# Router logits copied by ScalarE, gate factors stored by rows behind the rows' stores, the last routing ahead of the first expert slot, and solved systems back in four transfers

## The chip, the cores and the metric

The kernel runs on one core of a Trainium2 chip. The time is device microseconds for one execution, taken as the median of several runs. TensorE (PE) does the matmuls, VectorE (DVE), ScalarE (ACT) and GpSimd (POOL) the elementwise work, and SyncE (SP), ScalarE and GpSimd issue the DMA transfers, which 16 DMA engines carry out. The engines run their instructions in the order of the program and wait for one another by semaphores.

## What is computed

Three stages follow one another: a delta-rule attention over 768 steps for 4 x 8 heads of 48, a two-layer network with squared ReLU, and a mixture of eight experts of which each token takes the one with the highest router logit. Cut to its core:

```python
for t in range(S):                                   # attention, S = 768, D = 48
    kt, vt, bt = (k_n[:, :, t], v[:, :, t], beta[:, :, t, None])
    y[:, :, t] = np.einsum('bhd,bhde->bhe', q[:, :, t], state)
    v_old = np.einsum('bhde,bhd->bhe', state, kt)
    state = state + bt[:, :, :, None] * np.einsum('bhd,bhe->bhde', kt, vt - v_old)

x = y.transpose(0, 2, 1, 3).reshape(3072, 384)
h = np.maximum(x @ w_in, 0.0)                        # first network, d_ff = 2048
x = h * h @ w_out

logits = x @ w_gate                                  # experts: E = 8, F = 1024
expert_idx = np.argmax(logits, axis=1)
gate_w = softmax(logits)[np.arange(N), expert_idx]
for e in range(E):
    mask = expert_idx == e
    out[mask] = gate_w[mask, None] * (np.maximum(x[mask] @ w1[e], 0.0) @ w2[e])
```

## The kernel before

The 768 steps are cut into 12 chunks of 64. Within a chunk the recurrence becomes two triangular systems of 32 steps per head, which are solved for all 32 heads side by side. The order of all instructions is fixed when the program is built: a main loop runs over the chunks `c` and, in each, over eight units `i` of the first network (`l1_unit`, `l2_unit`), and hangs steps of the other work between them by tables of due times (in sixteenths of a chunk's units; `PRE_AT`, `CHAIN_AT`, `ROUTE_AT`).

While chunk `c` goes through the network, two other chunks are prepared. `pre(c)` consists of `front` and `solve`. `front` turns keys and queries, forms the Gram matrices (`grams`, L392 and L393, PSUM tile `gm`), and carries the 32 x 32 diagonal blocks through DRAM into a layout with one system per partition: ScalarE issues four stores `dg<-gd` (L422), SyncE two loads `gl<-dg` (L430). `solve` runs 31 elimination steps on VectorE (L520, L525), stores the result (`dt<-pt`, L535, two transfers) and loads it back by head (`tt<-dt`, L545, eight transfers of 32 KB). `norms` (L504) brings the key norms by head with small matmuls against columns of the unit matrix. `chain(c)` then does the sequential part: it loads `ktok` (L284), and runs z, u and y matmuls (L583, L594, L610); `s_step` (L641) updates the state at the start of the next chunk and reads `ktok`.

`route(c)` follows when the second layer of chunk `c` is done. It copies the rows out of PSUM (`xr`, L724, ScalarE) and stores them to DRAM (`xs_d`, L727, four transfers on SyncE); turns them (L734), multiplies them by the router's weights (L742, PSUM tile `lp`, 8 columns), copies the logits into the table `lga` (L743, VectorE, one for each of two token tiles), finds each token's expert and, by the rank matmuls `rk` (L781 to L785), its place in the expert's list, and scatters the token's number into `list_d` (L793, GpSimd). `gates(c0, c1)` turns logits into gate factors (`ga`, one per partition and column) and stores them to `g_d` (L809, four transfers on SyncE, in which each element of 4 bytes goes to its own place).

The PSUM tiles `gm`, `lp`, `xp`, `z`, `u`, `y` and `rk` share one pool of four buffers in turn.

In the last chunk the experts begin. At `i == 0` `first_slots` picks the two fullest lists, the lists of two slots are loaded (`ids`, L1017), the first slot's weights follow (`raw`, L992 and L996, seven transfers, 3 MB), and the gate factors of chunks 0 to 9 are stored. At `i == 2` GpSimd gathers the rows of the two slots (`gather`, L1023, `xg<-xs_d`) and their gate factors (`gather_gate`, L1032). A gather waits for all stores to its table that stand before it in the program. Weights are split into a high and a low part by ScalarE (L972) and VectorE (L973), `split_w`; each raw buffer that this frees takes the next slot's load.

After the loop the first slot's rows are turned (`transposed`, L1045, then L1047 on ScalarE and L1048 on VectorE, high and low part `xgT`), `route(11)` begins, and `slot(0)` and `slot(1)` run: four units of first-layer groups `h` (L1059, 18 matmuls of 256 columns) and second-layer groups `y` (L1071, 12 matmuls of 384 columns). The rest of `route(11)` is spread over slot 0, at `i == 2` the last two chunks' gate factors are stored and the third slot's list is loaded and its rows and factors gathered (`ahead(0)`); slot 1 also computes the table of the later slots (`slot_table`). Slots 2 to 9 are then one branch each, wide (L1081, L1091) or narrow.

The lines that move the transfers in question:

```python
for u in range(2):                                   # solve, L541 to L545
    for hf in range(2):
        for x in range(2):
            r0 = quad(x, hf)
            (nc.gpsimd if c == 0 and x else nc.sync).dma_start(out=tt[r0:r0 + 32, u], in_=dtr[hf, x, u])
```

## Time and profile before

| what | value |
|---|---|
| median of 3 runs | 1021.74 us (1018.74 to 1023.69) |
| the profiled execution | 1019.3 us, span 1017.5 us |
| mean granted clock of TensorE | 0.957 of full |
| busy: PE, PEld (its weight loads) | 910.4 us (89%), 849.9 us (84%) |
| busy: DVE, ACT, POOL | 664.9 us (65%), 514.3 us (51%), 315.4 us (31%) |
| DMA, mean over the span | 113.82 MB, 112 GB/s |
| packets under 512 bytes | 241053 of 273021 |

The table is read from the top: one engine, TensorE, is busy in nearly nine tenths of the span, so the time is its work plus what it stands still or runs slowly. The first 100 us are a start-up in which VectorE and the transfers set the pace, from there to about 711 us runs the loop over the chunks, then the experts. "SPq" in the rows is SyncE's queue of DMA issues and "ACTq" ScalarE's; a row gives the start, the duration, the engine, the source line, the operation, the tiles (out<-in) with their shapes, how many instructions the row holds, and in brackets how long the engine stood idle before it and what released it.

### The profile page before, as it was taken

What the parts mean: (1) busy time and instruction counts of PE and PEld (TensorE: products, weight loads), DVE (VectorE), ACT (ScalarE), POOL (GpSimd) and SP (SyncE); (2) the same over time, 40 slices, a digit from 0 to 9 for tenths busy, and PEclk for the clock granted to TensorE, in tenths of its full rate; (3) what the DMA queues carried; (4) which work ended last, traced back from release to release, by engine and by line L of the source; (5) the groups of instructions that cost most, each with busy time, mean ns of one, the idle gap of its engine ahead of it and who ended that gap; (6) DMA issues with size and microseconds to landing.
All of it is one profiled execution on the core that took longest, in us unless ns stands there. A gap on an engine that the chain in (4) does not pass through costs nothing.

```text
span 1017.5 us, 28821 instructions
## 1 busy us (share of the span) xinstructions
PE 910.4 (89%) x11416; PEld 849.9 (84%) x11416; DVE 664.9 (65%) x2270; ACT 514.3 (51%) x1025; POOL 315.4 (31%) x322
## 2 busy tenths in 40 slices
PE   6267979999899999999999999999789999999995
PEld 5135868988898888888888988999779999998994
DVE  6987897584949495868686777424564554463653
ACT  5146755555354645454545555455444444464553
POOL 2020023333142424242424342210434334353231
PEclk9689889999899999999999999999899999999998
DMA  8899292535343443435342531218786555564764
GB/s 159 139 184 272 40 103 31 84 38 85 49 83 50 77 56 57 61 57 74 63 72 49 80 55 38 38 55 140 139 251 209 158 165 174 165 218 136 236 199 133
DMA packets 273021, 113.82 MB, mean 112 GB/s; under 512 B 241053, under 2 KB 259554, under 8 KB 272096
## 3 DMA queue, kind: packets, MB, share of 16 engines
q1 hardware_dynamic: 244176, 92.87, 43.3%
q0 software_dynamic: 7344, 15.17, 5.8%
q10 hardware_dynamic: 21344, 3.67, 2.2%
q8 instruction: 100, 1.64, 0.8%
q14 instruction: 57, 0.47, 0.2%
HBM read 95.01 MB, written 17.82 MB: 111 GB/s over the span
## 4 chain that ended last, share of the span: by engine, by line
PE 54%; DVE 18%; DMA 12%; issue 5%; SPq 5%; ACT 4%; POOL 1%; another core or an unknown queue 0%; ACTq 0%; DVEq 0%; POOLq 0%
PE h L682 12%; PE x L710 11%; PE h L1059 6%; PE y L1071 5%; DVE tmp L520 5%; DVE pt L525 4%; PE h L1081 4%; PE y L1091 3%; DVE kq L381 2%; DMA raw<-in_moe_w_dram 2%; PE gm L392 2%; DMA xs_d<-xr 2%; PE wa L1091 2%; DMA st<-in_q_dram 1%; DMA xg<-xs_d,ids 1%
## 5 line engine op out<-in xcount | busy, mean ns | idle before, releaser
L682 PE MATMUL h<-xt,win 128*128 128x256 f32 x1728 | 235.1, 291 | 6.0 <-issue 2.9
L710 PE MATMUL x<-wout,gt 128*128 128x384 f32 x1152 | 229.1, 347 | 2.7 <-issue 2.3
L682 PEld LDWEIGHTS h<-xt,win 128*128 128x128 f32 x1728 | 220.6, 195 | 12.4 <-issue 5.1
L710 PEld LDWEIGHTS x<-wout,gt 128*128 128x128 f32 x1152 | 200.9, 192 | 9.7 <-issue 6.9
L692 POOL TENSOR_TENSOR gt<-r,gt 128x512 fp32r<-128x512 f32 x80 | 103.7, 1296 | 320.5 <-ACT gt L688 216.5
L520 DVE TENSOR_TENSOR tmp<-pt,gl 128x60 f32<-128x60 f32 (+37 forms) x662 | 142.4, 254 | 1.8
L686 ACT ACTIVATE r<-h 128x512 f32<-128x512 f32 x96 | 57.4, 597 | 166.9 <-PE h L682 118.9
L525 DVE TENSOR_TENSOR pt<-pt,tmp 128x60 f32<-128x60 f32 (+37 forms) x662 | 135.1, 243 | 4.3 <-remote 3.0
L973 DVE TENSOR_TENSOR ew<-raw,ew 128x768 fp32r<-128x768 f32 (+1 forms) x98 | 102.3, 1069 | 9.2 <-ACT ew L972 8.5
L1059 PE MATMUL h<-xgT,ew 128*128 128x256 f32 x648 | 85.0, 287 | 7.5 <-issue 4.5
L1059 PEld LDWEIGHTS h<-xgT,ew 128*128 128x128 f32 x648 | 82.1, 195 | 9.8 <-issue 7.3
L972 ACT CAST ew<-raw 128x768 fp32r<-128x768 f32 (+1 forms) x98 | 87.4, 923 | 1.9 <-DMA raw<-in_moe_w_dram 1.9
L1071 PE MATMUL y<-ew,ht 128*128 128x384 f32 x432 | 86.3, 347 | 0.0
L1071 PEld LDWEIGHTS y<-ew,ht 128*128 128x128 f32 x432 | 75.7, 193 | 0.1
L1101 POOL DMA_INDIRECT out_dram<-yo,ids x30 | 30.2, 1005 | 127.3 <-ACT yo L1100 119.2
L1063 DVE SCALAR_TENSOR_TENSOR ht<-h,ht 128x512 fp32r<-128x512 f32 x36 | 24.8, 690 | 65.9 <-ACT ht L1062 65.8
L1023 POOL DMA_INDIRECT xg<-xs_d,ids x36 | 44.2, 1229 | 71.5 <-DVE ew L973 42.6
L687 ACT ACTIVATE r<-r 128x512 f32<-128x512 f32 x96 | 60.7, 632 | 3.0
L688 ACT CAST gt<-r 128x512 fp32r<-128x512 f32 x96 | 59.6, 620 | 5.0 <-ACT r L687 0.4
L401 POOL TENSOR_TENSOR kq<-kq,qmask 64x256 f32<-64x256 f32 x72 | 53.4, 742 | 23.0 <-ACT kq L400 18.8
L597 ACT COPY sw<-u 32x384 f32<-32x384 f32 x96 | 45.1, 470 | 23.9 <-PE u L594 21.9
L392 PE MATMUL gm<-kq 48*64 48x128 f32 (+1 forms) x384 | 47.3, 266 | 7.1 <-DVE lga L743 5.4
(229 smaller groups left out, 1354.4 us busy)
## 6 DMA issues: line engine op xcount, KB each, us to landing
raw<-in_moe_w_dram SPq DMA_DIRECT2D x45, 512.0 KB
raw<-in_moe_w_dram SPq DMA_DIRECT2D x60, 384.0 KB
gl<-dg SPq DMA_DIRECT2D x24, 256.0 KB
rawo<-in_moe_w_out_dram SPq DMA_DIRECT2D x8, 768.0 KB
xs_d<-xr SPq DMA_DIRECT2D x48, 96.0 KB
ktok<-in_k_dram SPq DMA_DIRECT2D x22, 192.0 KB
dt<-pt SPq DMA_DIRECT2D x24, 128.0 KB
tt<-dt SPq DMA_DIRECT2D x92, 32.0 KB
```

The costliest lines, as they stand in the source:

```text
L392: nc.tensor.matmul(gm[64:128, j, c0:c1], kq[0:D, 0, r, 0:CH], kq[0:D, 0, r, c0:c1], start=True, stop=True)
L520: nc.vector.tensor_tensor(out=tv, in0=pt[:, js, s:s + 1].to_broadcast([P, m, n]), in1=gl[:, s:s + 1, s + 1:32].to_broadcast([P, m, n]), op ...
L525: nc.vector.tensor_tensor(out=pt[:, js, s + 1:32], in0=pt[:, js, s + 1:32], in1=tv, op=ALU.subtract)
L682: nc.tensor.matmul(h[:, f2], win_t[kk, half][:, wl, f0:f0 + P], xt[:, xl, kk], start=(n == 0), stop=(n == 3 * KD - 1))
L687: nc.scalar.activation(r, r, AF.Square)
L688: nc.scalar.copy(gt[:, 0], r)
L692: eng.tensor_tensor(out=gt[:, 1], in0=r, in1=gt[:, 0], op=ALU.subtract)
L710: nc.tensor.matmul(x2_t[c][t], gt[:, gl_, f2, ts_], wout_t[i][:, wl, f2], start=(f == 0 and n == 0), stop=(f == NF - 1 and n == 2),)
L972: nc.scalar.copy(dst[:, 0], raw)
L973: nc.vector.tensor_tensor(out=dst[:, 1], in0=raw, in1=dst[:, 0], op=ALU.subtract)
L1059: nc.tensor.matmul(h[:, f2], a[kk][:, wl, f * P:f * P + P], xgT[:, xl, kk, 0:SLOT], start=(n == 0), stop=(n == 3 * KD - 1))
L1071: nc.tensor.matmul(y, ht[:, hl, f2, ts_], b[i][:, wl, f2], start=(f == 0 and n == 0), stop=(f == NF2 - 1 and n == 2),)
```

## The change

The logits of chunks 0 to 10 are copied from PSUM by ScalarE instead of VectorE. `gates` sums into another order of columns, then turns the factors on TensorE (`gp`), copies them with ScalarE (`gT`) and stores rows of 64 factors, 10 or 2 rows a transfer; it becomes two steps. In the last chunk the first step stands where `gates` stood, the row gathers stay at `i == 2`, and the second step and the gathers of factors come at `i == 3`. In slot 0 the two halves stand at `i == 2` and `i == 3` in the same way, the third slot's list and row gather between them. `route(11)` begins before the first slot's rows are turned, copies its rows by VectorE, and its second step follows directly.

The 64 systems get another order over the partitions, so that the two halves of a head's chunk lie side by side in DRAM. That changes the views of `dg`, the columns in `norms`, and the load of beta (eight transfers for four), and lets `tt` come back in four transfers of 64 KB. For chunks 3 and later `chain` gets one more step, which holds the load of `ktok` alone and is due at 4.6 instead of 7.

```diff
@@ bounce
-            dgv = dg.rearrange("(u r two) s t -> u two s r t", u=2, two=2)
+            dgv = dg.rearrange("(r u two) s t -> u two s r t", u=2, two=2)
@@ norms
-                        r0, l0 = quad(x, hf), 32 * u + 16 * hf
-                        nc.tensor.matmul(nps[r0:r0 + 32, HP * u:HP * u + HP], nl[0:64, part[n]], ident[0:64, l0 + x:l0 + 16:2], start=True, stop=True)
+                        r0, l0 = quad(x, hf), 32 * hf + 2 * u + x
+                        nc.tensor.matmul(nps[r0:r0 + 32, HP * u:HP * u + HP], nl[0:64, part[n]], ident[0:64, l0:32 * hf + 32:4], start=True, stop=True)
@@ solve
-            tt = ap_.tile([P, 2, HP, 32], F32, tag="tt", bufs=2, name=f"tt{c}")
+            tt = ap_.tile([P, HP, 2, 32], F32, tag="tt", bufs=2, name=f"tt{c}")
             tt_t[c] = tt
-            dtr = dt.rearrange("(u f r two) j t -> f two u j r t", u=2, f=2, two=2)
-            for u in range(2):
-                for hf in range(2):
-                    for x in range(2):
-                        r0 = quad(x, hf)
-                        (nc.gpsimd if c == 0 and x else nc.sync).dma_start(out=tt[r0:r0 + 32, u], in_=dtr[hf, x, u])
+            dtr = dt.rearrange("(f r two) j t -> f two j r t", f=2, two=2)
+            for hf in range(2):
+                for x in range(2):
+                    r0 = quad(x, hf)
+                    (nc.gpsimd if c == 0 and x else nc.sync).dma_start(
+                        out=tt[r0:r0 + 32].rearrange("p r u t -> p (r u) t"), in_=dtr[hf, x],
+                    )
@@ chain
             load_k(c, ktok)
-        if c == 0:
+        if c == 0 or c > 2:
             yield
...
-                    nc.tensor.matmul(ut[o:o + 32, j], tt[o:o + 32, u, j], vt[o:o + 32, u, j], start=True, stop=True)
+                    nc.tensor.matmul(ut[o:o + 32, j], tt[o:o + 32, j, u], vt[o:o + 32, u, j], start=True, stop=True)
@@ route
-            nc.scalar.activation(xr, x2p[t], AF.Copy, scale=2.0 ** -LIFT)
+            if c == NCH - 1:
+                nc.vector.tensor_scalar(xr, x2p[t], 2.0 ** -LIFT, None, op0=ALU.mult)
+            else:
+                nc.scalar.activation(xr, x2p[t], AF.Copy, scale=2.0 ** -LIFT)
...
-            nc.vector.tensor_copy(lg[:, t], lp)
+            (nc.vector.tensor_copy if fast else nc.scalar.copy)(lg[:, t], lp)
@@ gates
-        nc.vector.tensor_reduce(out=ga, in_=lf, axis=AX.X, op=ALU.add)
+        nc.vector.tensor_reduce(out=ga.rearrange("p (t c) -> p c t", t=2), in_=lga[:, c0:c1], axis=AX.X, op=ALU.add)
         nc.vector.tensor_scalar(ga, ga, 1e-9, None, op0=ALU.add)
         nc.vector.reciprocal(ga, ga)
-        gv = ga.rearrange("p (c t) -> p t c", t=2)
+        yield
+        gp = ps_a.tile([n, P], F32, tag="a", name="gp")
+        nc.tensor.transpose(gp, ga, ident)
+        gT = p2.tile([n, P], F32, bufs=1, name=f"gT{c0}")
+        nc.scalar.copy(gT, gp)
+        m = c1 - c0
         for b in range(NB):
             nc.sync.dma_start(
-                out=g_d[b * S + c0 * CH:b * S + c1 * CH, :].rearrange("(c p) o -> p (c o)", p=CH),
-                in_=gv[64 * (b % 2):64 * (b % 2) + 64, b // 2],
+                out=g_d[b * S + c0 * CH:b * S + c1 * CH, :].rearrange("(c p) o -> c (p o)", p=CH),
+                in_=gT[b // 2 * m:b // 2 * m + m, 64 * (b % 2):64 * (b % 2) + 64],
             )
@@ load_bl
-                r0 = 64 * par + 32 * u
-                nc.gpsimd.dma_start(out=bl[r0:r0 + 32], in_=bf[:, :, u, :])
+                for x in range(2):
+                    r0 = 64 * par + 2 * u + x
+                    nc.gpsimd.dma_start(out=bl[r0:64 * par + 64:4], in_=bf[x::2, :, u, :])
@@ due times
+    CHAIN.update({c: (c - 1, (4.6,) + SCHED["CHAIN_AT"]) for c in range(3, NCH)})
@@ main loop, last chunk
         if c == NCH - 1 and i == 0:
-            gates(0, NCH - 2)
+            ga_steps = gates(0, NCH - 2)
+            advance(ga_steps)
         if c == NCH - 1 and i == 2:
+            gx.update({n: gather(n, ids[n]) for n in range(NFS)})
+        if c == NCH - 1 and i == 3:
+            run(ga_steps)
             for n in range(NFS):
-                gx[n] = gather(n, ids[n]) + (gather_gate(n, ids[n]),)
+                gx[n] += (gather_gate(n, ids[n]),)
@@ after the loop
+    last = route(NCH - 1)
+    advance(last)
     xT_next, todo = transposed(0)
     for t in todo:
         t()
-    last = route(NCH - 1)
     advance(last)
...
+    gb_steps = gates(NCH - 2, NCH)
@@ slot
-            if s == 0:
-                if i == 2:
-                    run(last)
-                    gates(NCH - 2, NCH)
-                    ahead(0)
+            if s == 0 and i == 2:
+                run(last)
+                advance(gb_steps)
+                gx[2] = gather(2, load_ids(2))
+            if s == 0 and i == 3:
+                run(gb_steps)
+                gx[2] += (gather_gate(2, gx[2][0]),)
```

Three places show what moves. SyncE in the last chunk, from the last of the first slot's weights (`raw`) to the first of the second's; `g_d` takes the gate factors, `xs_d` the rows of chunk 10. Before:

```order
L996 DMA raw_10658<-in_moe_w_dram 128x2x384
L809 DMA g_d<-ga_10697 64x10x1 x4
L727 DMA xs_d<-xr_10743 64x384 x2
L727 DMA xs_d<-xr_10747 64x384 x2
L992 ISA
L992 DMA raw_10952<-in_moe_w_dram 128x1024
```

and now:

```order
L1008 DMA raw_10614<-in_moe_w_dram 128x2x384
L731 DMA xs_d<-xr_10695 64x384 x2
L731 DMA xs_d<-xr_10699 64x384 x2
L818 DMA g_d<-gT_10804 10x64 x4
L1004 ISA
L1004 DMA raw_10912<-in_moe_w_dram 128x1024
```

The rows' stores have changed places with the gate factors' stores, which are now 10 rows of 64 instead of 64 rows of 10 single elements.

VectorE at the end of the loop, from the last unit's low part (`gt`) to the first slot's; `xr` are rows of chunk 11 out of PSUM, `ew` weights. Before:

```order
L692 TENSOR_TENSOR gt<-r,gt 128x512
L973 TENSOR_TENSOR ew_2_11046<-raw_10650,ew_2_11046 128x1024
L973 TENSOR_TENSOR ew_0_11062<-raw_10652,ew_0_11062 128x768
L973 TENSOR_TENSOR ew_1_11078<-raw_10654,ew_1_11078 128x768
L1048 TENSOR_TENSOR xgT_11082<-xp_0_11083,xgT_11082 128x3x128
L1048 TENSOR_TENSOR xgT_11082<-xp_1_11089,xgT_11082 128x3x128
L973 TENSOR_TENSOR ew_2_11103<-raw_10656,ew_2_11103 128x768
L973 TENSOR_TENSOR ew_3_11107<-raw_10658,ew_3_11107 128x768
L1063 SCALAR_TENSOR_TENSOR ht_11152<-h_0_11133,ht_11152 128x512
L973 TENSOR_TENSOR ew_3_11167<-raw_10952,ew_3_11167 128x1024
```

and now:

```order
L985 TENSOR_TENSOR ew_1_11038<-raw_10610,ew_1_11038 128x768
L726 TENSOR_SCALAR xr_11042<-x_0_10728 128x384
L726 TENSOR_SCALAR xr_11046<-x_1_10729 128x384
L1060 TENSOR_TENSOR xgT_11050<-xp_0_11051,xgT_11050 128x3x128
L1060 TENSOR_TENSOR xgT_11050<-xp_1_11057,xgT_11050 128x3x128
L985 TENSOR_TENSOR ew_2_11075<-raw_10612,ew_2_11075 128x768
L985 TENSOR_TENSOR ew_3_11079<-raw_10614,ew_3_11079 128x768
L1075 SCALAR_TENSOR_TENSOR ht_11124<-h_0_11105,ht_11124 128x512
L747 COPY lga<-lp 128x8 x2
L773 TENSOR_REDUCE sm<-lga 128x2
```

The two copies of `xr` stand ahead of `xgT`, and the logits of the last routing come after the first `ht` (before, two more weight splits and the second `ht` came first).

ScalarE in a chunk of the loop, between the Gram copies (`gd`, `kq`) and the turned rows (`x2T`). Before:

```order
L400 COPY kq_130<-gm 64x4x64
L408 COPY kq_130<-gm 32x4x32
L736 COPY x2T<-xp 128x384
L395 COPY gd_6395<-gm 128x256
L400 COPY kq_131<-gm 64x4x64
```

and now:

```order
L400 COPY kq_130<-gm 64x4x64
L408 COPY kq_130<-gm 32x4x32
L747 COPY lga<-lp 128x8
L740 COPY x2T<-xp 128x384
L395 COPY gd_6371<-gm 128x256
L400 COPY kq_131<-gm 64x4x64
```

The copy of the logits stands in ScalarE's row, ahead of the second turned tile; VectorE's row has lost it. A second one follows later in the chunk, behind a group of `r` and `gt` and ahead of the four copies `sw`.

## Rows read from the trace of the kernel before

**Rows 1.** PE's waits over the span: total us, times, longest us.

```profile
PE xp L1045 <- DMA xg<-xs_d,ids: 9.4, 3, 5.5
...
PE gm L392 <- DVE lga L743: 5.4, 5, 1.3
...
PE u L594 <- DMA tt<-dt: 1.2, 2, 0.7
...
PE h L1059 <- DVE xgT L1048: 0.9, 1, 0.9
```

**Rows 2.** Timeline of one chunk in the loop, 498 to 524 us, all engines.

```profile
498.22 0.32 PE L392 MATMUL gm<-kq 48*64 48x128 f32 x1 [1.22 <-DVE lga L743]
...
501.71 2.83 ACTq L422 DMA_DIRECT2D dg<-gd  x2
...
504.35 0.17 DVE L743 COPY lga<-lp 128x8 f32<-128x8 f32 x1 [5.72 <-PE lp L742]
...
509.54 0.18 PE L781 MATMUL rk<-ohb,triu 128*128 128x8 bf16 x1
...
523.10 0.18 ACT L506 COPY ncol<-nps 128x16 f32<-128x16 f32 x1
```

**Rows 3.** Timeline of SyncE's queue, 680 to 775 us.

```profile
685.34 7.74 SPq L809 DMA_DIRECT2D g_d<-ga  x4
693.18 8.04 SPq L727 DMA_DIRECT2D xs_d<-xr  x4
...
745.80 0.39 SPq L1017 DMA_DIRECT2D ids<-list_d  x1
```

**Rows 4.** Stretches of 2 us: busy PE, PEld, DVE, ACT, POOL; PEclk, DMA share, GB/s.

```profile
694.00:696.00 2.00, 2.00 (x20) 2.00 (x19) 0.12 (x1) 0.29 (x1) 0.00 (x0) 1.00 1.03 33
...
716.00:718.00 2.00, 1.17 (x6) 1.14 (x6) 0.00 (x0) 0.23 (x1) 1.58 (x2) 0.50 0.25 51
...
762.00:764.00 2.00, 2.00 (x8) 1.90 (x8) 0.56 (x1) 0.48 (x1) 1.64 (x2) 0.50 0.28 99
```

**Rows 5.** Timeline of GpSimd, 680 to 775 us.

```profile
711.03 0.99 POOL L1023 DMA_INDIRECT xg<-xs_d,ids  x1 [42.59 <-DVE ew L973]
...
735.82 1.07 POOL L793 DMA_INDIRECT list_d<-tid,pos  x1 [0.30 <-issue]
750.95 2.73 POOL L1023 DMA_INDIRECT xg<-xs_d,ids  x1 [14.06 <-issue]
```

**Rows 6.** Timeline of PE, 655 to 775 us.

```profile
704.92 6.41 PE L710 MATMUL x<-wout,gt 128*128 128x384 f32 x36
716.83 1.54 PE L1045 MATMUL xp<-ident,xg 128*128 128x128 f32 x6 [5.49 <-DMA xg<-xs_d,ids]
...
722.98 0.82 PE L734 MATMUL xp<-ident,xr 128*128 128x128 f32 x6
...
725.74 1.40 PE L742 MATMUL lp<-wg,x2T 128*128 128x8 f32 x12
...
758.78 0.55 PE L1045 MATMUL xp<-ident,xg 128*128 128x128 f32 x3 [3.18 <-DMA xg<-xs_d,ids]
...
768.10 4.48 PE L1059 MATMUL h<-xgT,ew 128*128 128x256 f32 x36 [0.23 <-issue]
```

**Rows 7.** Chain that ended last, from 774 us: start, us, what.

```profile
774.66 2.11 PE h L1059 x18
```

**Rows 8.** Timeline of VectorE at the first slot's start.

```profile
718.28 1.20 DVE L1048 TENSOR_TENSOR xgT<-xp,xgT 128x384 fp32r<-128x384 f32 x2 [7.29 <-ACT xgT L1047]
```

**Rows 9.** Timeline of SyncE's queue in the same chunk as rows 2.

```profile
501.74 3.81 SPq L545 DMA_DIRECT2D tt<-dt  x8
505.65 1.36 SPq L284 DMA_DIRECT2D ktok<-in_k_dram  x2
```

**Rows 10.** Timeline of the start-up, GpSimd and VectorE.

```profile
4.47 2.69 POOL L829 DMA_DIRECT2D bl<-in_beta_dram  x4
...
29.55 0.22 DVE L487 TENSOR_TENSOR cc<-s,bl 128x64 f32<-128x64 f32 x1
```

## The prediction

> **What bounds the kernel now.** I read PE's waits over the whole span first [rows 1]. TensorE is the engine that everything feeds, so what it waited for by name is what can be won back. Two entries belong to code that the change touches: 9.4 us until a gather of token rows (xg) had landed, in three waits, and 5.4 us in five waits of the first-stage loop, where a Gram matmul (gm) waited for VectorE's copy of the router logits (lga). The transfer tt, which the change halves in number, cost 1.2 us in all.
>
> Then the loop, in one chunk [rows 2]: gm starts at 498.22 after 1.22 us idle, released by that copy. VectorE reaches the 8-column copy only behind a long run of solve steps, and until then the PSUM buffer that gm wants stays taken. One level down, ScalarE sits in the issue of its last two dg stores for 2.83 us (501.71).
>
> Then the passage from the first stage to the experts. SyncE needs 7.74 us to issue the four stores of gate factors [rows 3]: one element of 4 bytes each, 2560 in all. In that time the DMA engines are full and move 33 GB/s [rows 4]. The stores of the rows themselves (xs_d) stand behind them, from 693.18, and the first gather, which needs those rows, is issued only at 711.03 [rows 5]. TensorE ends its last L2 group at 704.92 + 6.41 = 711.33 and stands still for 5.49 us [rows 6]. Then it runs at a granted clock of 0.50 (1.2 instead of 2.4 GHz) [rows 4]. The same repeats at the third slot: its list of tokens is loaded at 745.80 [rows 3], its gather is issued at 750.95 after 14.06 us idle of GpSimd [rows 5], TensorE waits 3.18 us at 758.78 [rows 6] and again falls to 0.50 [rows 4].
>
> **The passage, in numbers.** From 711.33 to the first matmul of the third slot at 768.10 [rows 6] are 56.8 us. The work in it at full clock: eight groups h at 2.11 [rows 7] make 16.9; eight groups y of twelve matmuls, at 6.41 / 36 each [rows 6], make 17.1; 27 transposes at 0.82 for six make 3.7; the router matmuls 1.4 [rows 6]; the few small ones I put at 0.6. Sum 39.7. So 17.1 us are waits and half clock.
>
> What of it stays? In the changed order the xs_d stores follow the weight loads directly, at about 685 where the gate stores began. The loads are over before the element stores fill the engines at 694 [rows 4], so the rows should land near 694. GpSimd, idle for 42.59 us before 711, issues the four row gathers then, 0.99 us each and a short gap [rows 5]; with the 5.8 us that the first took from issue to its transpose at 716.83 they are in by 705, six us before TensorE asks. The first stall and its half clock go.
>
> In its place a smaller one comes. The last routing now stands ahead of the first slot: after the six transposes of the gather PE does six more of xr. VectorE copies xr from PSUM, two tiles of the size for which it takes 1.20 us in a pair [rows 8], and only then subtracts the low halves of xgT, another 1.20, which the second matmul of h needs. So h begins some 2.2 us after 711.33, at 713.5; 1.5 of that are transposes, 0.7 to 1.0 is idle. I keep the 0.9 us that h waited for xgT in the second slot [rows 1] and 0.4 for a router result that is asked for one group earlier. Left over: about 2.1 us. **Gain in the passage: 17.1 - 2.1 = 15.0 us.**
>
> The third slot's gather decides whether that holds. Before, from the router matmuls at 725.74 to the end of the list's scatter at 735.82 + 1.07 are 11.2 us [rows 5, 6]; one y pair of 2.1 leaves that path, so 9.1. Now the router matmuls run at 713.5 + 2.1 = 715.6 and the scatter ends at 724.7. From there to the third slot's transpose took 736.89 to 758.78, 21.9 us. If nothing of that improved, the rows would be there at 746.6. PE needs them after eight h, six y, the router work, six transposes and the small waits: 713.5 + 16.9 + 12.8 + 1.4 + 0.6 + 0.8 + 1.3 = 747.3. That fits by 0.7 us, and the 512 element stores of the second gate write, which stood before the list's load on SyncE, now come behind it as eight short rows. So I count no wait, with a bound of 7 us (3.2 waited, the second and third tile, half clock after).
> The Trainium skill, "DMA: Bandwidth & Descriptors", section "Queues, rings and completion order", says that each DMA engine goes round the queues it has work for, packet by packet. By that rule a gather on GpSimd's queue takes turns with the weight loads instead of standing behind them, and the bound of 7 would hardly be reached; the trace does not settle it, for no gather ran alone there.
>
> **The logits by ScalarE.** 22 copies leave VectorE (0.17 us each [rows 2]) and 22 join ScalarE, whose nearest row, 16 columns from PSUM, took 0.18 us [rows 2]: 4.0 us of ScalarE's time, spread over eleven chunks, on an engine that is half idle. The first copy of a chunk stands right after the Gram copies, before x2T, which waits for a later transpose anyway. So PSUM is free some 5 us earlier and the five waits go: **5.4 us**. Bounds: 0 if another wait takes the place, 5.4 if none does; a gain beyond is excluded, since no other wait is named for that copy, and a loss only comes about as in the slower rival below. I take 5.4.
> The second copy stands behind a Relu group and ahead of four sw copies, so VectorE's eight small router steps start some 2 us later than at 504.35. Before them VectorE idled 5.72 us, and the rank matmul rk comes at 509.54 [rows 2], so about 1.5 us of slack is left.
> The Trainium skill, "Perfetto Trace Analysis", section "DVE / Act Engine Instruction", states that a small ScalarE copy runs about 2.3 times its specified time; by it one might fear 0.39 us per copy, 8.6 us in all. The row for 16 columns does not show that.
>
> **Four transfers for tt, ktok earlier.** SyncE's eight issues took 3.81 us and ktok's two 1.36 more, with the Gram load gl behind both [rows 9]. Four issues of twice the size should take about half; the packets, 128 bytes each, stay as many. ktok is now issued a few units earlier, when SyncE is idle, and waits only for the matmuls that read the old one, long done. tt lands some 1.9 us and gl some 3.3 us sooner. TensorE hardly waited for tt, so nothing is gained directly; but the loop now reaches u 1.2 us sooner, and the two just about cancel. I count 0, bounds -3 to +3: the dg stores that held ScalarE for 2.83 us take turns with fewer transfers.
>
> **At nothing:** eight beta loads for four on GpSimd. They took 2.69 us from 4.47; even doubled they are done before 12, and VectorE reads them at 29.55 [rows 10]. The weight loads behind them come up to 2.7 us later, into a stretch where VectorE and ScalarE still work on the first keys; uncovered it would cost those 2.7. The transposes gp with their ScalarE copies are two of each, under 1 us, and the gate gathers behind them are read only at a slot's end.
>
> **How the numbers follow.** 15.0 + 5.4 + 0 = 20.4 us. The profiled execution took 1019.3 us (span 1017.5), so 998.9; the median of before lies 2.4 above that execution, so the forecast on the median is 1021.7 - 20.4, **1001 us**.
>
> **Rivals.** *Third slot still late.* For: list, ids and gather keep three transfers in a row, and the weight loads crowd in now too. Against: the sum above. It takes back 7: 1008.
> *The loop finds another wait.* For: the tt chain starts at the end of VectorE's solve, which is no faster, so u may wait where gm did. Against: tt lands sooner by about as much. It takes back 5.4: 1007.
> *The row stores don't land earlier* (the change doesn't do what it says): they still queue behind 3 MB of weights and something else holds the gathers. Then only the loop and part of the second stall come: 5.4 + 3, 1013.
> *Slower:* ScalarE's second logits copy comes too late and rk, on TensorE in order, waits in every chunk, with h and x queued behind it. Slack is 1.5 us. To undo the gain of 20.4 it would have to cost 2 us in each of ten chunks, and to be slower by 0.5% 2.6, so the copy would come over 4 us later than I read. Then 1027 or more. Against: in each chunk of the trace VectorE idles for over 5 us there.
>
> Chances: forecast 0.60 (its own range 995 to 1006), third slot late 0.17, another wait in the loop 0.11, rows not earlier 0.08, slower 0.04. The first three are faster by over 0.5%, which is about what a measurement of this kernel can tell from no change; of the fourth I give 0.03 to faster and 0.05 to the same. Faster 0.91, same 0.05, slower 0.04. Range 994 to 1013: the low end adds the 3 us bound of tt and some of the smaller waits, the high end takes in the fourth case.
>
> **What would show it.** PE's waits should have no gm behind lga and no xp of 5 us; xs_d issued before 690 and the gathers before 700; the granted clock at 1.00 from 711 to 730; the third slot starting near 748 (768.1 less 20.4). A wait of xp at the third slot, or of rk or u in the loop, would say which rival holds. I would be wrong as a whole if the weights of the second slot became late, since its loads must now land in a slot shorter by some 3 us.

## The result, and the profile after

The changed kernel measured 1010.88 us (median of four, 1005.91 to 1014.38) beside 1020.24 for the kernel before: a ratio of 0.9883, 95% interval [0.9843, 0.9923], which is 11.9 us; the medians lie 9.4 apart. I had forecast 1001, a gain of 20.4. The direction and the range held; the size was about half. The profiled execution was the slowest of the four (span 1012.6 us).

PE's waits in the changed kernel, total us, times, longest us, answering to [rows 1]:

```profile
PE h L683 <- issue: 8.3, 5, 3.7
PE h L1071 <- issue: 7.7, 4, 2.5
PE x L711 <- issue: 7.6, 3, 6.4
...
PE u L595 <- DMA tt<-dt: 2.7, 6, 0.8
...
PE xp L1057 <- DMA xg<-xs_d,ids: 0.7, 1, 0.7
```

No gm waits for lga any more, and the gathers cost 0.7 us instead of 9.4. In their place stand u behind tt, 2.7 instead of 1.2, and waits of PE for "issue", for nothing that the profile names: 36.3 us over all lines against 23.4 before.

The passage in the changed kernel answers to [rows 3 to 6]. PE's timeline:

```profile
711.08 6.42 PE L711 MATMUL x<-wout,gt 128*128 128x384 f32 x36
...
719.46 2.25 PE L1071 MATMUL h<-xgT,ew 128*128 128x256 f32 x17 [0.29 <-DVE xgT L1060]
...
756.30 0.52 PE L1057 MATMUL xp<-ident,xg 128*128 128x128 f32 x3 [0.74 <-DMA xg<-xs_d,ids]
...
761.20 5.99 PE L1071 MATMUL h<-xgT,ew 128*128 128x256 f32 x36 [2.26 <-issue]
```

SyncE's queue in the same stretch:

```profile
691.63 3.13 SPq L731 DMA_DIRECT2D xs_d<-xr  x4
696.02 3.02 SPq L818 DMA_DIRECT2D g_d<-gT  x4
```

GpSimd's timeline, the first gather:

```profile
700.77 0.99 POOL L1035 DMA_INDIRECT xg<-xs_d,ids  x1 [25.76 <-DMA g_d<-gT]
```

Two stretches of 2 us, columns as in [rows 4]:

```profile
716.00:718.00 2.00, 2.00 (x16) 1.96 (x15) 2.00 (x4) 0.14 (x1) 0.00 (x0) 1.00 1.06 15
762.00:764.00 2.00, 2.00 (x13) 2.00 (x12) 0.00 (x0) 0.00 (x0) 0.73 (x1) 0.54 0.81 160
```

The last L2 group ends at 711.08 + 6.42 = 717.50, the third slot starts at 761.20: 43.7 us instead of 56.8. The rows' stores go out 25.9 us ahead of that end, the first gather 16.7 ahead, the first stall is gone and the clock stays at 1.00 there. At the third slot's start stands a new pause of 2.26 us with a stretch at 0.54 behind it. The gather's row names `g_d<-gT`, but by the semaphores in the trace the last of the rows' stores landed at 699.70, 1.07 us ahead of the gather; in the kernel before these two stand at 709.92 and 711.03, so it is still the rows that the gather waits for. Two of the forecast's signs, xs_d issued before 690 and the gathers before 700, were missed by 1.6 and 0.8 us, in a trace that loads the lists 6.4 us later (686.33 against 679.93).

### The profile page after: what moved, and what is told of

Same layout as the page of the kernel before. It is cut to its first block, busy times and chain, and to the rows that moved or that the text cites. A ratio compares the mean times of both kernels' runs of the same rounds, so it can differ in the third digit from the quotient of the medians.

```text
span 1012.6 us, 28787 instructions
## 1 busy us (share of the span) xinstructions
PE 908.4 (90%) x11418; PEld 849.7 (84%) x11418; DVE 677.2 (67%) x2250; ACT 515.7 (51%) x1047; POOL 318.2 (31%) x324
## 3 DMA queue, kind: packets, MB, share of 16 engines
q1 hardware_dynamic: 240336, 92.87, 42.4%
## 4 chain that ended last, share of the span: by engine, by line
PE 55%; DVE 18%; DMA 11%; issue 6%; ACT 4%; SPq 3%; POOL 1%; another core or an unknown queue 0%; ACTq 0%; DVEq 0%; POOLq 0%
PE h L683 12%; PE x L711 12%; PE h L1071 7%; DVE tmp L520 6%; PE y L1083 5%; DVE pt L525 5%; PE h L1093 4%; PE y L1103 3%; DVE kq L381 2%; DMA dt<-pt 2%; DMA vz<-in_v_dram 2%; DMA st<-in_q_dram 2%; PE wa L1103 2%; PE u L595 2%; DMA tt<-dt 1%
## 5 line engine op out<-in xcount | busy, mean ns | idle before, releaser
L683 PE MATMUL h<-xt,win 128*128 128x256 f32 x1728 | 231.9, 288 | 9.7 <-issue 8.3
L683 PEld LDWEIGHTS h<-xt,win 128*128 128x128 f32 x1728 | 217.8, 193 | 16.0 <-issue 10.7
L520 DVE TENSOR_TENSOR tmp<-pt,gl 128x60 f32<-128x60 f32 (+37 forms) x662 | 145.5, 259 | 1.8
L525 DVE TENSOR_TENSOR pt<-pt,tmp 128x60 f32<-128x60 f32 (+37 forms) x662 | 132.6, 239 | 5.4 <-remote 2.4
L1083 PE MATMUL y<-ew,ht 128*128 128x384 f32 x432 | 84.0, 341 | 0.0
L598 ACT COPY sw<-u 32x384 f32<-32x384 f32 x96 | 45.2, 471 | 50.7 <-PE u L595 48.9
L401 POOL TENSOR_TENSOR kq<-kq,qmask 64x256 f32<-64x256 f32 x72 | 53.4, 741 | 22.8 <-ACT kq L400 18.7
L1074 ACT ACTIVATE ht<-h 128x512 fp32r<-128x512 f32 x36 | 21.6, 599 | 62.5 <-PE h L1071 54.5
```

The costliest lines, as they stand in the source:

```text
L520: nc.vector.tensor_tensor(out=tv, in0=pt[:, js, s:s + 1].to_broadcast([P, m, n]), in1=gl[:, s:s + 1, s + 1:32].to_broadcast([P, m, n]), op ...
L525: nc.vector.tensor_tensor(out=pt[:, js, s + 1:32], in0=pt[:, js, s + 1:32], in1=tv, op=ALU.subtract)
L683: nc.tensor.matmul(h[:, f2], win_t[kk, half][:, wl, f0:f0 + P], xt[:, xl, kk], start=(n == 0), stop=(n == 3 * KD - 1))
L1083: nc.tensor.matmul(y, ht[:, hl, f2, ts_], b[i][:, wl, f2], start=(f == 0 and n == 0), stop=(f == NF2 - 1 and n == 2),)
```

## The experiments

They ran in three sets of four, each set on one chip beside the kernel before, whose median was 1006.65, 1009.22 and 1032.98 us. Ratios are therefore compared within a set first. Microseconds against the kernel before follow from the ratios, those between two runs of a set from the medians. The kernel before, as a run of its own, measured 0.9969 [0.9943, 0.9996] of itself: below some 0.4% I read nothing.

| run | what it is | ratio | 95% interval |
|---|---|---|---|
| again | the changed kernel | 0.9898 | 0.9853 to 0.9943 |
| logits | before + both copies of the logits on ScalarE | 1.0023 | 0.9992 to 1.0054 |
| passage | before + gate rows + last routing first | 0.9914 | 0.9881 to 0.9947 |
| systems | before + new order of the systems, four tt | 0.9994 | 0.9960 to 1.0027 |
| before_again | the kernel before | 0.9969 | 0.9943 to 0.9996 |
| logits_first | before + first copy alone on ScalarE | 0.9973 | 0.9945 to 1.0001 |
| rows_only | before + gate rows, routing order as before | 0.9906 | 0.9877 to 0.9935 |
| no_systems | changed, systems and tt as before | 0.9815 | 0.9776 to 0.9854 |
| after_eight | changed, tt in eight, first halves first | 0.9913 | 0.9880 to 0.9946 |
| no_ktok | no_systems, ktok where it was | 0.9939 | 0.9913 to 0.9964 |
| no_logits | no_systems, logits by VectorE | 0.9915 | 0.9881 to 0.9949 |
| best1 | no_systems, second logits copy by VectorE | 0.9861 | 0.9827 to 0.9894 |

### The parts one by one

**again**, the changed kernel unedited. 

> The changed kernel once more, for a second trace. In the first one PE waited 36.3 us for nothing that the profile names (the kernel before: 23.4), 6.4 us of it in one piece at 375.7, after which it ran 6.8 us at half clock. Theory A (these pauses are scatter: PE's instructions arrive late now and then): that pause is gone, the span is near 1005, and the start-up to 166 us may be anything from 0 to 7 us longer than before. Theory B (the pauses belong to the changed program): the same pauses stand at the same matmuls, span 1010 to 1013.

The span was 994.1 on a faster chip. Neither theory held as written: the unnamed waits fell to 25.1 us, the one of 6.4 us came back at the same matmuls with 4.42. The kernel before pauses there too (0.9 us, and 4.6 in its second trace). So the place is the program's and the length varies.

**passage**, all hunks of the change on gates, the last chunk, the slots and the last routing:

```diff
-                out=g_d[b * S + c0 * CH:b * S + c1 * CH, :].rearrange("(c p) o -> p (c o)", p=CH),
-                in_=gv[64 * (b % 2):64 * (b % 2) + 64, b // 2],
+                out=g_d[b * S + c0 * CH:b * S + c1 * CH, :].rearrange("(c p) o -> c (p o)", p=CH),
+                in_=gT[b // 2 * m:b // 2 * m + m, 64 * (b % 2):64 * (b % 2) + 64],
...
+    last = route(NCH - 1)
+    advance(last)
     xT_next, todo = transposed(0)
```

> The kernel before with the gate factors turned and stored by rows behind the rows' stores, and the last routing ahead of the first slot; logits, tt and ktok as before. My prediction's term: 15 us, 1006. From the first trace of the change: the passage from the last second-layer group to the third slot's first h took 43.9 us instead of 56.8, with a new wait of 2.3 us at the third slot's start, so 11 to 13 us: 1008 to 1010.

It was worth 8.7 us, and in its trace the passage took 42.4 us.

**systems**, the hunks of `bounce`, `norms`, `solve`, the u matmuls and `load_bl`:

```diff
-            tt = ap_.tile([P, 2, HP, 32], F32, tag="tt", bufs=2, name=f"tt{c}")
+            tt = ap_.tile([P, HP, 2, 32], F32, tag="tt", bufs=2, name=f"tt{c}")
...
-            dtr = dt.rearrange("(u f r two) j t -> f two u j r t", u=2, f=2, two=2)
+            dtr = dt.rearrange("(f r two) j t -> f two j r t", f=2, two=2)
```

> The kernel before with the new order of the 64 systems alone: four transfers for tt, eight for beta, norms and dg to match; ktok where it was. My prediction's term: 0 (bounds -3 to +3), 1021. Theory B from the first trace (the start-up grew by 7 us to 166 us because SyncE, done sooner with tt, puts the big weight loads into the stretch where PE's instructions and the first chunks' rows are fetched): 1025 to 1028, start of the third chunk's Gram matmuls 5 to 7 us later than 167.

No change in all. The first traces' 5 to 7 us at the start were partly scatter: the first state update `ku` begins at 82.0 to 85.0 us in the ten traces with the old order and at 84.8 to 87.6 in the four with the new one, by the medians 2.6 us later.

**logits**:

```diff
-            nc.vector.tensor_copy(lg[:, t], lp)
+            (nc.vector.tensor_copy if fast else nc.scalar.copy)(lg[:, t], lp)
```

> The kernel before with the copy of the logits by ScalarE and nothing else. My prediction's term: the five waits of gm for lga (5.4 us) go, 1016. Rival (another wait takes the place): the waits go but the chunks keep their length, 1020 to 1022.

The five gm waits went and the time did not. A new line stands among PE's waits:

```profile
PE rk L781 <- DVE ohb L774: 7.0, 7, 1.5
```

One chunk of that kernel, timeline of all engines:

```profile
499.05 1.34 ACTq L422 DMA_DIRECT2D dg<-gd  x2
...
502.31 0.16 ACT L743 COPY lga<-lp 128x8 f32<-128x8 f32 x1
...
502.50 0.17 DVE L769 TENSOR_REDUCE sm<-lga 128x2 f32<-128x16 f32 x1 [8.99 <-ACT lga L743]
...
502.53 1.29 POOL L692 TENSOR_TENSOR gt<-r,gt 128x512 fp32r<-128x512 f32 x1 [5.50 <-issue]
...
502.70 1.15 DVE L770 TENSOR_TENSOR lga<-lga,sm 128x16 f32<-128x16 f32 x1
...
504.74 0.17 PE L781 MATMUL rk<-ohb,triu 128*128 128x8 bf16 x1 [0.97 <-DVE ohb L774]
```

ScalarE sits in its last two dg issues until 500.39; the second copy of the logits, behind a Relu group, comes at 502.31 and starts VectorE's routing steps. Their subtraction takes 1.15 us instead of 0.17 and ends as GpSimd's product ends (503.85 and 503.82). Then rk, in order on TensorE, has waited 0.97 us. Seven such waits make 7.0 us for the 5.4 that went. This is the mechanism of my slower rival, at half the price.

### What the first trace had been

**before_again**, the kernel before unedited. 

> The kernel before once more, for a second trace of it. The first trace had a first gather 5.5 us late at 711 us and 0.9 us of pause at the twelve second-layer matmuls near 367; every other trace so far has 4.4 to 6.4 us at that place, and the runs of the two kernels that leave the passage alone show the first gather late by 0 and 2.8 us. If the first trace was typical, both numbers return. If they are scatter, the pause near 365 is 4 to 6 us and the first gather is late by 0 to 3 us, so that my 15 us for the passage were read from an unlucky execution.

PE's waits in that second trace:

```profile
PE x L710 <- issue: 4.9, 2, 4.6
...
PE xp L1045 <- DMA xg<-xs_d,ids: 2.8, 2, 1.5
```

Its passage, in PE's timeline:

```profile
696.82 6.41 PE L710 MATMUL x<-wout,gt 128*128 128x384 f32 x36
...
755.06 4.44 PE L1059 MATMUL h<-xgT,ew 128*128 128x256 f32 x36 [1.29 <-ACT yo L1100]
```

The gathers cost 2.8 us, not 9.4, and the passage took 755.06 - 703.23 = 51.8 us, not 56.8. In the other three traces that leave the passage alone it took 48.1 to 51.9. The first trace was an unlucky execution for the passage, and the pause near 365 us, 0.9 there, is 4.6 here.

**rows_only**, the edit of passage without the earlier routing, so that this order stays:

```diff
     xT_next, todo = transposed(0)
     for t in todo:
         t()
     last = route(NCH - 1)
...
+    gb_steps = gates(NCH - 2, NCH)
```

> The kernel before with the gate factors turned and stored by rows, behind the rows' stores, and the last routing where it was (behind the turning of the first slot's rows). The whole passage measured 0.9914 of before, 8.7 us. Theory A (the element stores held everything): most of it is here, 6 to 9 us, and the third slot's gather still comes 1 to 4 us late in all. Theory B (the earlier routing is what counts): 2 to 4 us here, the rest in the order.

It was worth 9.5 us, with a passage of 41.4 us, beside 8.7 for **passage** in another set. So all of it is in the gate factors' stores: the earlier routing adds nothing that can be measured, and the third slot's gather comes in time without it (0.2 us of waits). This edit changes both the stores' form and their place behind the rows' stores; neither by itself was tried.

**logits_first**:

```diff
-            nc.vector.tensor_copy(lg[:, t], lp)
+            (nc.vector.tensor_copy if fast or t else nc.scalar.copy)(lg[:, t], lp)
```

> The kernel before with only the first of a chunk's two copies of the logits on ScalarE, the second on VectorE as it was. With both on ScalarE the gm waits went, but the rank matmuls rk waited 0.5 to 1.5 us in seven chunks, because the second copy comes behind gt, which also starts GpSimd's product, and VectorE's next step (lga minus its maximum) then takes 1.14 us instead of 0.17. Theory A (that is what ate the 5.4 us): no gm<-lga wait, no rk wait, the subtraction at 0.17, and 4 to 6 us faster than before. Theory B (the chunk's length is set elsewhere, by tt or by the arrival of PE's instructions): the waits go and the time stays within 2 us of before.

There is no gm wait and no rk wait, and the subtraction takes 0.17. The gain is 2.7 us, which the interval does not part from nothing. By itself this leaves the term open; best1 below says more.

**no_systems**, the changed kernel with every hunk of **systems** undone:

```diff
-            tt = ap_.tile([P, HP, 2, 32], F32, tag="tt", bufs=2, name=f"tt{c}")
+            tt = ap_.tile([P, 2, HP, 32], F32, tag="tt", bufs=2, name=f"tt{c}")
```

> The changed kernel without the new order of the systems: tt in eight transfers, beta in four, the rest as changed, ktok early too. If the systems cost what two traces show up to 170 us (3 to 4 us, a pause of 3 to 4 us at the first h group near 84 us), this is 2 to 4 us faster than the changed kernel, 0.985 to 0.988 of before. If four transfers for tt earn in the loop what they lose at the start (u waited for tt there), it is the same as the changed kernel, 0.990.

It measured 0.9815, a gain of 18.7 us, near the 20.4 that I had forecast for the whole change. Its loop shows a part of why. First the changed kernel (run again), one chunk, timeline of SyncE's queue:

```profile
493.38 1.26 SPq L535 DMA_DIRECT2D dt<-pt  x2
...
497.71 1.94 SPq L544 DMA_DIRECT2D tt<-dt  x4
```

PE's weight loads of the first u group in the same chunk:

```profile
500.35 0.13 PEld L595 LDWEIGHTS u<-vz,tt 32*32 32x32 f32 x2 [0.25 <-ACT lga L747]
501.10 0.13 PEld L595 LDWEIGHTS u<-vz,tt 32*32 32x32 f32 x2 [0.62 <-DMA tt<-dt]
501.40 0.13 PEld L595 LDWEIGHTS u<-vz,tt 32*32 32x32 f32 x2 [0.17 <-DMA tt<-dt]
```

Then no_systems, one chunk, timeline of all engines:

```profile
489.24 1.25 SPq L535 DMA_DIRECT2D dt<-pt  x2
...
491.67 1.97 ACTq L422 DMA_DIRECT2D dg<-gd  x2
...
493.31 3.79 SPq L545 DMA_DIRECT2D tt<-dt  x8
...
495.77 0.16 ACT L746 COPY lga<-lp 128x8 f32<-128x8 f32 x1
...
496.58 1.16 PE L594 MATMUL u<-vz,tt 32*32 32x48 f32 x64
...
499.92 0.18 PE L784 MATMUL rk<-ohb,triu 128*128 128x8 bf16 x1
```

And the kernel before, in the chunk of [rows 2]:

```profile
498.12 1.25 SPq L535 DMA_DIRECT2D dt<-pt  x2
...
506.47 0.88 PE L594 MATMUL u<-vz,tt 32*32 32x48 f32 x64
```

In the first, u is reached 500.35 - 493.38 = 7.0 us after the issue of dt and stands waiting for tt until 8.0. Over the run u's matmuls waited 2.4 us for tt and their weight loads (PEld) 4.4:

```profile
PEld u L595 <- DMA tt<-dt: 4.4, 12, 0.8
...
PE u L595 <- DMA tt<-dt: 2.4, 5, 0.6
```

Matmuls and weight loads mostly waited at the same time (two rows of one wait), so the 17 pieces cover 4.4 us of time, 1.4 in the start-up and 3.1 in the loop; counted one by one they make 6.9, the number that the expectation of after_eight below uses. In the second u is reached after 7.3 us, before all eight transfers of tt are issued, and does not wait for tt in the whole run. In the kernel before u came 8.4 us after the issue of dt. With four transfers each carries both halves of a chunk, so the first u group needs all of them.

### Taking the rest apart

In the third set the u matmuls of all four traces pause for "issue", for 13.9 to 15.5 us in 33 to 40 pieces, which none of the other ten traces shows; all four ratios lie higher than expected, so they are compared with one another alone.

**after_eight**:

```diff
-            for hf in range(2):
-                for x in range(2):
-                    r0 = quad(x, hf)
...
-                        out=tt[r0:r0 + 32].rearrange("p r u t -> p (r u) t"), in_=dtr[hf, x],
...
+            for u in range(2):
+                for hf in range(2):
+                    for x in range(2):
+                        r0 = quad(x, hf)
+                        (nc.gpsimd if c == 0 and x else nc.sync).dma_start(out=tt[r0:r0 + 32, :, u], in_=dtr[hf, x][:, u::2])
```

> The changed kernel with all of it, the new order of the systems included, but tt loaded in eight transfers again, those for the first half of every head's chunk first. The version without the new order measured 0.9815 of before, the changed kernel 0.9898; in its trace u waited 6.9 us for tt, in the other not at all. Theory A (with four transfers each carries both halves, so the first u matmuls wait for twice the bytes): no u<-tt wait in the loop, the chunks near 49.5 us as without the new order, 0.982 to 0.985. Theory B (the new order itself costs, by its stores of dg, its eight loads of beta or the start-up): chunks near 50.9 us, 0.989 to 0.991.

PE's waits there:

```profile
PE u L594 <- issue: 15.5, 40, 0.5
...
PE u L594 <- DMA tt<-dt: 0.8, 2, 0.5
```

The waits for tt in the loop are gone; that part of theory A holds. Two late chunks (Gram matmuls at 500.28 and 604.42) average 52.1 us, as in best1 (52.1), but no_ktok, 8.6 us behind best1, has 51.8 there, so these chunks do not part the versions. The total fits theory B, 5.4 us behind best1's median, with intervals that overlap a little. In the two traces 2.0 us stand in the start-up (third chunk's Gram matmuls at 170.66 against 168.65; the ten traces with the old order have 166.2 to 171.6); the rest is open.

**no_ktok**, in no_systems:

```diff
-        if c == 0 or c > 2:
+        if c == 0:
             yield
...
-    CHAIN.update({c: (c - 1, (4.6,) + SCHED["CHAIN_AT"]) for c in range(3, NCH)})
```

> The version without the new order of the systems, and with ktok loaded where it was: the passage and both copies of the logits on ScalarE. In the trace of the logits alone rk waited 1.0 us a chunk, ScalarE sat in its last two dg issues until 500.4 and copied the second logits at 502.3; with ktok early there was no rk wait. Theory A (the early ktok frees the lanes that the dg stores wait for, and the logits only pay with it): rk waits of about 1 us are back and the time is 0.990 to 0.993. Theory B (ktok does nothing, as I counted): 0.981 to 0.984, as with it.

One chunk of it, timeline of all engines:

```profile
512.03 0.53 ACTq L422 DMA_DIRECT2D dg<-gd  x1
...
516.05 1.34 ACTq L422 DMA_DIRECT2D dg<-gd  x2
...
519.30 0.16 ACT L746 COPY lga<-lp 128x8 f32<-128x8 f32 x1
...
521.73 0.17 PE L784 MATMUL rk<-ohb,triu 128*128 128x8 bf16 x1 [0.95 <-DVE ohb L777]
```

ScalarE's first row behind the dg issues, here and then in no_systems:

```profile
517.49 0.60 ACT L686 ACTIVATE r<-h 128x512 f32<-128x512 f32 x1 [4.75 <-DMA tt<-dt]
```

```profile
493.95 0.60 ACT L686 ACTIVATE r<-h 128x512 f32<-128x512 f32 x1 [2.19 <-DMA dg<-gd]
```

The rk waits are back (6.3 us, seven times; in no_systems there was none). The last two dg issues come 4 us after the first two; with ktok early they follow at once (491.67 in no_systems), and the second logits copy, there 0.8 us ahead of u, comes here 1.75 after it began. The trace names what holds dg: the two late issues wait for semaphores that transfers of tt raise when they land, at 516.02 and 517.05, and start 0.03 and 0.02 us later. In each of the seven traces with ktok late and tt in eight transfers, 11 or 12 issues of dg from 180 us on are held so; with four transfers (systems) it is 3, and in the six traces with ktok early at most one. The edit does not touch dg; what it changes is which earlier transfer dg has to wait for.

**no_logits**, in no_systems:

```diff
-            (nc.vector.tensor_copy if fast else nc.scalar.copy)(lg[:, t], lp)
+            nc.vector.tensor_copy(lg[:, t], lp)
```

> The version without the new order of the systems, and with the logits copied by VectorE as before: the passage and the early ktok. My term for the logits is 5.4 us. Theory A (the term holds once tt and ktok don't stand in its way): gm waits of 1.0 to 1.25 us in five to seven chunks, 5 to 6 us slower than the version with the copies on ScalarE, 0.986 to 0.988. Theory B (the early ktok alone made the loop shorter): 0.981 to 0.983.

Theory A held in its waits:

```profile
PE gm L392 <- DVE lga L746: 5.8, 6, 1.0
```

The median is 7.6 us behind best1's (5.6 by the ratios, whose intervals overlap a little).

**best1**, in no_systems:

```diff
-            (nc.vector.tensor_copy if fast else nc.scalar.copy)(lg[:, t], lp)
+            (nc.vector.tensor_copy if fast or t else nc.scalar.copy)(lg[:, t], lp)
```

> The passage, the early ktok, no new order of the systems, and of the two copies of the logits only the first on ScalarE. VectorE's routing steps start some 2 us earlier and without the 1 us in which they stand behind GpSimd's product. If rk had no slack left in the version with both copies on ScalarE, this is 1 to 4 us faster than that one, 0.978 to 0.981; if it had (no rk wait stands in its trace), the same, 0.981 to 0.983.

It is the fastest of its set, by 5 to 9 us. Against no_systems it was not run in one set, so whether the second copy matters once ktok is early is open. That the change without the new order of the systems beats the changed kernel is likely and not shown (0.9815 against 0.9883 and 0.9898, from different sets, with intervals that overlap or touch at their ends).

## Why the prediction was right in direction and half wrong in size

**Passage, 15.0: mis-sized, 8.7 measured.** The end state was right: I had 39.7 us of work and 2.1 of waits, 41.8 in all, and the nine traces with the new stores show 40.7 to 43.7. What failed is the minuend: "from 711.33 to the first matmul of the third slot are 56.8 us" was one execution, and the four other traces without the new stores have 48.1 to 51.9, a mean of 50.7 against 41.7 in the nine with them. The rival of the third slot's late gather did not come (0.7 us). I had h at 2.2 us after the last L2 group; its first matmul came at 1.3, its second at 719.46 - 717.50 = 2.0. The third slot I had put at 748: it came at 761.2, since the last L2 group ended at 717.5 and not at 705.9 (711.3 less the loop's 5.4), and 1.9 us of passage came on top. The earlier routing, which I had counted as part of the remedy, was not needed.

**Logits, 5.4: nothing alone, about its size with ktok early.** The waits went as said, but the step "about 1.5 us of slack is left" at rk failed: I had not seen that the subtraction would stand behind GpSimd's product for 0.97 us, nor that ScalarE's held dg issues come ahead of the second copy. Alone the edit gave nothing (1.0023). With ktok early rk has slack again (ohb is ready at 498.1 in no_systems, rk comes at 499.92): with both copies on ScalarE, the two traces with ktok late have seven rk waits each and the four with it early have none. Then the edit seems to pay: 7.6 us between no_logits and best1, which moves the first copy only.

**tt and ktok, 0: two terms of opposite sign that I had put into one.** I gave ktok no part in the gain, and the logits' second copy hangs on it: no_ktok is 8.6 us behind best1, which differs in that copy too. The new order of the systems with its four transfers seems to cost the changed kernel about 8 us (0.9898 against 0.9815). The two ratios come from two sets, and in the second the kernel before measured 0.9969 of itself, so 5 us fit as well. The step that failed is "tt lands some 1.9 us sooner": SyncE was done sooner, but the first u needed twice the bytes. "The loop now reaches u 1.2 us sooner" was right (7.0 us after the issue of dt in again, 8.4 before), and so the rival of another wait in the loop came true, by at most 3.1 us in the loop of again where I had priced it at 5.4. That systems alone cost nothing fits: there gm still waits 5.3 us in all, and u comes later by that. The traces of again and no_systems lie 9.7 us apart: 2.0 ahead of the first state update (84.84 and 82.83), 4.1 from there to the end of the last L2 group, of which u's waits are at most 3.1, and 3.6 behind it, where both kernels do the same work. So in these two traces at most some 6 are the new order's; its start-up and what after_eight left open are not explained.

**At nothing:** the transposes and rows of gate factors did cost nothing that shows. The eight beta loads came with the new order of the systems, whose start-up is about 2 us longer; what part is theirs was not tried.

## What to carry to other kernels

A stall read from one execution is a sample: before subtracting it, see whether other traces of the same code have it. When transfers are merged, ask which bytes the first reader needs; fewer issues do not help it if each transfer now also carries what is read last. A copy that changes engines also changes what it starts: look at what runs beside the next instruction. And a transfer that changes its place can change which earlier transfer another one waits for: look at what released the issue that comes late.

## What the runs showed of the hardware

**VectorE behind GpSimd.** The subtraction of 16 columns took 0.17 to 0.18 us in every chunk of the kernel before and 1.12 to 1.15 in the first ten chunks of each kernel with both copies on ScalarE, always ending 0.03 us behind GpSimd's product gt, while the reduction ahead of it, with one input, ran at 0.17 beside that product. In the last two routings, with no product of GpSimd beside it, it took 0.17 to 0.19; where VectorE kept the second copy it took 0.17 to 0.20 throughout. The Trainium skill, "SBUF — State Buffer", section "SBUF: two separate sides", says that a VectorE operation with two SBUF inputs and a GpSimd operation that reads SBUF exclude each other for the whole instruction; these rows agree.
ScalarE's copy of 8 columns out of PSUM took 0.16 to 0.17 us and VectorE's 0.15 to 0.17, so the 0.39 us that the prediction feared did not come. The Trainium skill's factor of 2.3 ("Perfetto Trace Analysis", section "DVE / Act Engine Instruction (TENSOR_ADD, Activation, etc)") is one against a specified time, for operands in SBUF and 128 elements; the prediction multiplied a measured copy by it, and no run here shows such a copy.

**Row packets behind element stores.** In [rows 4] the DMA engines are full at 33 GB/s, and the prediction put that down to the element stores alone. Packet by packet, some 2300 of the 2560 packets of 4 bytes started between 690 and 694 us and took 9 to 12 ns each on the mean. What fills the engines most from 694 to 700 are 116 of the 256 row packets of 1536 bytes behind them, at 717 to 801 ns each by stretches of 2 us; packets of that size took 65 to 73 ns in the changed kernel from 692 to 700. The element stores were still not through: the first, issued at 685.34, landed at 704.85. Why the row packets took ten times as long stays open.

**Pauses that no engine causes.** All fourteen traces have 17 to 36 us in which PE waits for nothing named, and thirteen pause at the second-layer matmuls near 365 us (they resume at 360 to 378), for 0.9 to 6.4 us. The longest in the changed kernel, PE's timeline:

```profile
375.74 3.04 PE L711 MATMUL x<-wout,gt 128*128 128x384 f32 x9 [6.42 <-issue]
```

The instruction queues' packets from 361 to 373 us (packets, MB, share of 16 engines):

```profile
q14 instruction: 1, 0.01, 0.2%
```

and from 373 to 375 us:

```profile
q8 instruction: 1, 0.02, 2.9%
```

The stretch behind it, columns as in [rows 4]:

```profile
376.00:378.00 2.00, 2.00 (x8) 2.00 (x8) 1.96 (x7) 0.00 (x0) 0.00 (x0) 0.50 0.50 73
```

In the twelve microseconds up to 373, in whose course PE ran dry, no packet came on q8; after one of 16 KB had come, PE went on, at half clock. In all thirteen traces PE resumed 1.0 to 1.5 us after the end of such a packet. They number 100 in every trace, about one for 228 of PE's 22832 or 22836 matmuls and weight loads. The Trainium skill, "Runtime: NRT & Kernel Launch", section "Instruction fetch mechanics", says that instructions are refilled in blocks of 16 KB, at a cost that is mostly hidden; the size agrees, the cost here was 6.4 us and the half clock. Why the packet came late, and why at this place, stays open.
